# Attention and two expert layers on one core: merged q, k and v loads, another order of products at layer ends, silu in one operation

## Chip, cores and metric

One core of a Trainium2 chip runs the whole program in one launch. The metric is device time in microseconds (us), as the median of several executions.

## What is computed

```python
scores = scale * q @ k.T - log(S)          # (4, 12, 448, 64) each of q, k, v
attn   = 1 / (1 + exp(-scores))
x      = attn @ v                          # -> (1792, 768) rows: batch x sequence
xn     = x / sqrt(mean(x*x) + 1e-6) * rms_g
x      = (silu(xn @ w_gate) * (xn @ w_val)) @ w_out      # d_ff 1536
h      = x @ w_in
out    = (h - tanh(h)) @ w_out2                          # d_ff 2048
```

All arrays are fp32. The kernel splits every fp32 operand into a high and a low fp32r part and makes each product from three matmuls (high·high, high·low, low·high).

## The kernel before

**Stages.** Activations lie with features on the 128 partitions and the 448 tokens of one batch element along the free dimension. The attention works through 24 pairs of heads (4 batch elements, 6 pairs each). For a pair, `pair_load` (L490 to L520) brings q, k and v; `pair_prep` splits q and k (L279, L530); `scores` (L553) makes the scores of two heads in the two halves of the partitions; `sigmoid` (L563) is eight ScalarE operations; `pair_av` (L593, L599) multiplies by v, and `pair_end` copies the result out. After six pairs `norm` (L634, L644) works out the root mean square of a batch element.

Then come two layers, first for the batch elements 0 and 1 together, then for 2 and 3. The first matrix of a layer (phases Ag and Av for gate and value, C for the second layer) is multiplied by Strassen-Winograd's seven products over two rows of blocks and two batch elements: one *job* (`seven_units`, matmuls at L794) has 7 products of 3 steps `i` of 3 matmuls, 63 in all, and takes six PSUM banks; product 2 goes on top of product 1's bank. Step `i` needs the right-hand operands of feature chunks 2i and 2i+1 (B11, B21, B22 and the sums T1 to T4), which `right_units` makes (L675 sums, L279 and L670 split). `end` turns the results into activations: for the gate a ScalarE sigmoid (L742) and a multiplication by the value itself (L743), on VectorE or GpSimd. The second matrix (phases B and D, matmuls at L830) adds up groups of GR = 4 rows `k` of blocks over six columns `m`, a group of 4 jobs and 144 matmuls; `epilogue` (L721) adds each group's sum to an accumulator. The last group of phase B also calls `right_units` for phase C.

**Weights.** They come as int64 words holding an fp64 value; `load` (L317) fetches 768 KB, `convert` makes fp32 of it (ScalarE L333, L338, L342, then a clamp L345 and a shift-and-or L347), `factors` makes the sums (L413) and splits (L418) for a job, `whole_tile` the splits for B and D (L459). Converted weights are stored to DRAM for the second pass. The first six jobs' weights are converted beside the attention.

**What sets the order.** All work is recorded as units in a list; `Plan.issue` then simulates the five queues with written-down durations and takes, among the units that can start soonest (within 300 ns), the one recorded first. So each engine's instruction order is fixed when the program is built, and each engine runs it in order: an instruction that waits holds up all behind it, on SP (all DMA issues) too. The order of the blocks in B and D is the list `ORDER_1_OUT` or `ORDER_2_OUT`; in a job the order is this (L805 to L810, first job of a phase: `p == 0`):

```python
names = (1, 6, 7, 5, 2, 4, 3)
if p == 0:
    order = [(n, i) for n in names[:4] for i in range(2)] + [(n, 2) for n in names[:4]]
    order += [(n, i) for n in names[4:] for i in range(3)]
```

`right_a` (L868) makes the right-hand operands of phase A; for the second pass its units are spread beside the last jobs of the first one, where x is read back from DRAM. L279 is the helper `copy`, used for casts and for copies out of PSUM.

## Time and profile before

| what | us |
|---|---|
| median of 3 executions (1157.83 to 1166.39) | 1160.0 |
| the profiled execution | 1158.56 |
| its span, first to last instruction | 1156.8 |
| TensorE busy (96% of the span, 5574 records) | 1107.9 |
| VectorE busy (75%) | 865.2 |
| ScalarE busy (48%) | 558.2 |
| GpSimd busy (28%) | 321.9 |

The mean granted TensorE clock is 0.984 of full speed. A row of a timeline gives the start, the time taken, the engine, the source line, what it does and how many instructions were merged; in brackets stands the idle time ahead of it and what ended it. "SPq" is the queue that issues all DMAs. A few matmul records are missing from the trace, so a count there can be some short.

### The profile page before, as it was taken

What the parts mean: (1) busy time and instruction counts of PE and PEld (TensorE: products, weight loads), DVE (VectorE), ACT (ScalarE), POOL (GpSimd) and SP (SyncE); (2) the same over time, 40 slices, a digit from 0 to 9 for tenths busy, and PEclk for the clock granted to TensorE, in tenths of its full rate; (3) what the DMA queues carried; (4) which work ended last, traced back from release to release, by engine and by line L of the source; (5) the groups of instructions that cost most, each with busy time, mean ns of one, the idle gap of its engine ahead of it and who ended that gap; (6) DMA issues with size and microseconds to landing.
All of it is one profiled execution on the core that took longest, in us unless ns stands there. A gap on an engine that the chain in (4) does not pass through costs nothing. (4 is left out here: it accounts for less than half of the span.)

```text
span 1156.8 us, 15127 instructions
## 1 busy us (share of the span) xinstructions
PE 1107.9 (96%) x5574; PEld 943.8 (82%) x5574; DVE 865.2 (75%) x1347; ACT 558.2 (48%) x904; POOL 321.9 (28%) x203
## 2 busy tenths in 40 slices
PE   8798988999999997999999899999999999999998
PEld 4344443989999986899999789999999899999987
DVE  2566883796698899898999899948838899394642
ACT  4678996455476576676575424312303243121110
POOL 0003010253254232334444523322211324051300
PEclk9898999999999999999999899999999999999999
DMA  3777655234257463455556651221313113313203
GB/s 105 228 216 235 195 152 190 91 109 164 82 191 269 141 232 123 138 211 198 207 211 216 241 189 56 83 82 55 110 55 110 55 56 109 104 61 110 109 1 123
DMA packets 55322, 162.27 MB, mean 140 GB/s; under 512 B 13904, under 2 KB 30928, under 8 KB 55248
## 3 DMA queue, kind: packets, MB, share of 16 engines
q1 hardware_dynamic: 55248, 161.30, 41.4%
q8 instruction: 44, 0.72, 0.3%
q14 instruction: 30, 0.25, 0.1%
HBM read 115.27 MB, written 46.01 MB: 139 GB/s over the span
## 5 line engine op out<-in xcount | busy, mean ns | idle before, releaser
L794 PE MATMUL ps<-unit,wt 128*128 128x448 f32 x2160 | 454.9, 368 | 11.2 <-DVE unit L670 7.0
L794 PEld LDWEIGHTS ps<-unit,wt 128*128 128x128 f32 x2160 | 407.8, 189 | 49.6 <-DVE unit L670 7.8
L830 PE MATMUL ps<-unit,wt 128*128 128x448 f32 x2016 | 416.6, 367 | 8.2 <-DVE unit L279 7.3
L830 PEld LDWEIGHTS ps<-unit,wt 128*128 128x128 f32 x2016 | 379.7, 189 | 42.8 <-DVE unit L279 8.4
L765 DVE TENSOR_TENSOR unit<-ps,unit 128x448 f32<-128x448 f32 x240 | 142.6, 618 | 47.5 <-PE ps L794 44.0
L279 ACT COPY unit<-ps 128x448 f32<-128x448 f32 x86 | 45.8, 534 | 162.5 <-PE ps L794 90.0
L279 ACT CAST unit<-unit 128x448 fp32r<-128x448 f32 (+1 forms) x143 | 76.9, 567 | 86.0 <-DVE unit L721 22.0
L721 DVE TENSOR_TENSOR unit<-ps,unit 128x448 f32<-128x448 f32 x120 | 68.9, 616 | 60.9 <-PE ps L830 60.8
L345 POOL TENSOR_SCALAR cv<-cv 128x768 f32<-128x768 f32 x28 | 82.6, 2948 | 89.1 <-ACT cv L342 89.1
L563 ACT ACTIVATE unit<-ps 128x448 f32<-128x448 f32 x192 | 90.2, 543 | 5.4 <-PE ps L553 4.1
L279 ACT CAST wt<-cv 128x768 fp32r<-128x768 f32 x78 | 64.6, 833 | 57.2 <-PE ps L794 20.8
L553 PE MATMUL ps<-unit 64*128 64x448 f32 (+1 forms) x576 | 75.7, 397 | 14.3 <-ACT unit L279 5.0
L553 PEld LDWEIGHTS ps<-unit 64*128 64x128 f32 (+1 forms) x576 | 52.1, 182 | 42.9 <-issue 18.8
L794 PE MATMUL ps<-unit,cv 128*128 128x448 f32 x360 | 79.8, 366 | 0.0
L593 PE MATMUL ps<-unit 128*64 128x448 f32 x288 | 68.2, 607 | 9.3 <-ACT unit L563 9.2
L794 PEld LDWEIGHTS ps<-unit,cv 128*128 128x128 f32 x360 | 67.5, 188 | 5.6
L708 DVE TENSOR_TENSOR unit<-unit 128x448 fp32r<-128x448 f32 x89 | 66.5, 757 | 4.3 <-ACT unit L279 2.3
L418 POOL TENSOR_TENSOR wt<-cv,wt 128x768 fp32r<-128x768 f32 x21 | 41.6, 1980 | 100.2 <-ACT wt L279 56.7
L279 DVE CAST unit<-unit 128x448 fp32r<-128x448 f32 (+1 forms) x102 | 48.2, 473 | 28.2 <-DMA unit<-in_qkt 25.4
L342 ACT ACTIVATE cv<-wt 128x768 f32<-128x768 f32 x68 | 61.5, 906 | 10.5 <-DVE cv L347 3.9
L708 POOL TENSOR_TENSOR unit<-unit 128x448 fp32r<-128x448 f32 x23 | 26.8, 1169 | 138.0 <-DVE unit L279 130.2
L418 DVE TENSOR_TENSOR wt<-cv,wt 128x768 fp32r<-128x768 f32 x59 | 62.1, 1064 | 2.5 <-ACT wt L279 1.5
(71 smaller groups left out, 1020.7 us busy)
## 6 DMA issues: line engine op xcount, KB each, us to landing
wt<-in_w_out SPq DMA_DIRECT2D x28, 768.0 KB, 4.9
wt<-in_w_in SPq DMA_DIRECT2D x16, 768.0 KB, 5.9
wD<-wt SPq DMA_DIRECT2D x16, 768.0 KB, 4.1
wt<-wD SPq DMA_DIRECT2D x16, 768.0 KB, 4.2
wt<-in_w_gate SPq DMA_DIRECT2D x12, 768.0 KB, 5.4
wt<-in_w_val SPq DMA_DIRECT2D x12, 768.0 KB, 5.8
wB<-wt SPq DMA_DIRECT2D x12, 768.0 KB, 4.0
wt<-wB SPq DMA_DIRECT2D x12, 768.0 KB, 4.1
```

The costliest lines, as they stand in the source:

```text
L279: add(engines, lambda e: (nc.scalar.copy if e == "ACT" else nc.vector.tensor_copy)(to(), of()), reads, writes)
L342: add(act(NW), lambda e: nc.scalar.activation(t.tile, r.tile[:, :, 1].bitcast(F32), AF.Abs, scale=2.0 ** 16), [r["h"]], [t["t"]])
L345: add({**dve(NW, fast=True), **pool1(NW)}, lambda e: ENG[e].tensor_scalar(out=t.tile, in0=t.tile, scalar1=LOW, scalar2=HIGH, op0=ALU.max, ...
L418: add({**dve(n, psum=False), **pool(n)}, lambda e: ENG[e].tensor_sub(lo(), a(), hi().bitcast(F32)), [*ak, kh], [kl])
L553: nc.tensor.matmul(ps[i, c].tile[:n, :S], lhsT=f[w].tile[rows, c * P:c * P + n], rhs=f[q].tile[rows, :], start=(w, q) == ("kh", "qh"), sto ...
L563: add(act(S, psum=True), lambda e: nc.scalar.activation(to.tile[at:at + n, :S], ps.tile[:n, :S], AF.Sigmoid, bias=-math.log(S), scale=1.0 ...
L593: nc.tensor.matmul(ps.tile[i * D:(i + 1) * D, :S], lhsT=v.tile[:, n * D:(n + 1) * D], rhs=a.tile, start=(c == 0), stop=False)
L708: add({**pool(S), **dve(S, psum=False)}, lambda e: ENG[e].tensor_sub(c["l"].tile, t.tile, c["h"].tile.bitcast(F32)), [t["t"], kh], [kl])
L721: add(dve(S), lambda e: nc.vector.tensor_add(a.tile, psv(), a.tile), [ps["t"], a["t"]], [a["t"]])
L765: add(dve(S), lambda e: nc.vector.tensor_add(t.tile, banks[n].tile[:, :S], x.tile), [banks[n]["t"], x["t"]], [t["t"]])
L794: nc.tensor.matmul(ps.tile[:, :S], lhsT=part(a), rhs=x[b].tile, start=n not in ON_TOP and i == 0 and q == 0, stop=i == 2 and q == 2, skip_ ...
L830: nc.tensor.matmul(ps.tile[:, :S], lhsT=wt, rhs=a[p].tile, start=first and i == 0, stop=last and i == 2,)
```

## The change

- q and k of two heads are read as one DMA of 128 rows instead of two of 64; only the last 64 columns of k in batch elements 0 and 1 stay apart. v of a pair is one DMA for its first three chunks and one for the last. In batch elements 0 and 1 the last chunk is now read with its zero half. The first two weight loads no longer wait for the third pair's operands; the plan counts 3500 instead of 2000 ns until a weight load has landed.
- In B and D the last group runs the first three columns with its first two rows, the same columns with its last two rows, then the other three columns with four rows each. In a phase's first job the steps 0 and 1 of the products 1, 6, 7, 5, 4 and 3 come first, then all that need step 2 and product 2.
- `right_units` is made in two parts, for an even and an odd chunk, and recorded 60 places earlier for the plan's choice (`plan.lag`). The second pass's `right_a` ends one job earlier.
- silu is one ScalarE `Silu`; the multiplication L743 for it is gone. The clamp (L345) is VectorE's alone. The pools change: 79 instead of 81 units, 6 instead of 5 conversion buffers, and one instead of two `c` tiles among them.

```diff
-N_UNIT, N_MOE, N_WT, N_CV = 81, 44, 8, 5
+N_UNIT, N_MOE, N_WT, N_CV = 79, 44, 8, 6
+FIRST = 60
+def out_order(n):
+    half = GR // 2
+    order = [(k, m) for g in range(n // GR - 1) for m in range(KM) for k in range(g * GR, (g + 1) * GR)]
+    order += [(k, m) for ks in (range(n - GR, n - half), range(n - half, n)) for m in range(KM // 2) for k in ks]
+    return order + [(k, m) for m in range(KM // 2, KM) for k in range(n - GR, n)]
-ORDER_1_OUT = [(k, m) for g in range(KF1 // GR) for m in range(KM) for k in range(g * GR, (g + 1) * GR)]
+ORDER_1_OUT = out_order(KF1)
...
+        self.rank.append(n + self.lag)
...
-            finish, start, n, e, ns, uses_port = min((c for c in cands if c[1] <= soonest), key=lambda c: c[2])
+            finish, start, n, e, ns, uses_port = min((c for c in cands if c[1] <= soonest), key=lambda c: (self.rank[c[2]], c[2]))
...
-        "cv": (N_CV, {"cv": 2, "c": 2, "top": 1, "a22": 2}),
+        "cv": (N_CV, {"cv": 2, "c": 1, "top": 1, "a22": 2}),
...
-        add({"SP": (2200, False)}, lambda e: nc.sync.dma_start(out=r.tile, in_=SRC[ph][at]), reads, [r["l"], r["h"]], after=2000)
+        add({"SP": (2200, False)}, lambda e: nc.sync.dma_start(out=r.tile, in_=SRC[ph][at]), reads, [r["l"], r["h"]], after=3500)
...
-            add({**dve(NW, fast=True), **pool1(NW)}, lambda e: ENG[e].tensor_scalar(
+            add(dve(NW, fast=True), lambda e: ENG[e].tensor_scalar(
...
-            for i in range(2):
-                rows = slice(i * D, (i + 1) * D)
-                of = qkt[b * H + 2 * p + i][rows]
...
-                add({"SP": (1.4 * (hi - lo), False)}, lambda e, of=of, rows=rows, at=at: nc.sync.dma_start(
+            apart = w == "k" and hi > 3 * P and b < PAIRED
+            for i in range(2 if apart else 1):
+                rows = slice(i * D, (i + 1) * D) if apart else slice(0, P)
+                of = qk_rows[h * P + D:][rows, at + i * D:at + i * D + hi - lo]
+                add({"SP": (640 if apart else max(460, 1.45 * (hi - lo)), False)}, lambda e, of=of, rows=rows: nc.sync.dma_start(
...
-                if b % 2 and m % 2:
-                    for u in right_units("C", (b - 1, b), m // 2, xg):
+                if b % 2:
+                    plan.lag = -FIRST
+                    for u in right_units("C", (b - 1, b), m // 2, xg, m % 2):
                         u()
+                    plan.lag = 0
...
-            add(act(S, psum=psum), lambda e: nc.scalar.activation(sg.tile, of(), AF.Sigmoid), [x["t"]], [sg["t"]])
-            add(two, lambda e: ENG[e].tensor_mul(sg.tile, of(), sg.tile), [x["t"], sg["t"]], [sg["t"]])
+            add(act(S, psum=psum), lambda e: nc.scalar.activation(sg.tile, of(), AF.Silu), [x["t"]], [sg["t"]])
...
-            order = [(n, i) for n in names[:4] for i in range(2)] + [(n, 2) for n in names[:4]]
-            order += [(n, i) for n in names[4:] for i in range(3)]
+            free = [n for n in names if n not in ON_TOP]
+            order = [(n, i) for n in free for i in range(2)]
+            order += [(n, i) for n in names for i in range(3) if i == 2 or n in ON_TOP]
...
-        load(i, [pair_t[0, BEHIND]["ql"][0]] if (0, BEHIND) in pair_t else [])
+        load(i)
...
-    beside = [(last_c + 1, half_way, right_a(BATCHES[1], True))]
+    beside = [(last_c + 1, half_way - 1, right_a(BATCHES[1], True))]
```

The queue of SP at the program's start, before the change; `in_qkt` holds q and k, `in_vp` v in pairs, `ve` the last chunk of v:

```order
L500 DMA unit<-in_qkt 64x128 x2
L500 DMA unit<-in_qkt 64x448 x2
L500 DMA unit<-in_qkt 64x256 x2
L500 DMA unit<-in_qkt 64x64 x2
L511 DMA unit<-in_vp 128x384
L520 DMA ve<-in_vp 64x64 x2
L500 DMA unit<-in_qkt 64x384 x2
L500 DMA unit<-in_qkt 64x64 x2
L500 DMA unit<-in_qkt 64x448 x2
```

And with it, as far as the second pair's q:

```order
L513 DMA unit<-in_qkt 128x128
L513 DMA unit<-in_qkt 128x448
L513 DMA unit<-in_qkt 128x256
L513 DMA unit<-in_qkt 64x64 x2
L531 DMA unit<-in_vp 128x384
L533 DMA ve<-in_vp 128x128
L513 DMA unit<-in_qkt 128x384
L513 DMA unit<-in_qkt 64x64 x2
L513 DMA unit<-in_qkt 128x448
```

Up to the second pair's q, SP issued seventeen DMAs; now it issues eleven.

ScalarE around the last score sigmoids (L563 before, L576 now); L742 is the gate's sigmoid, L766 the gate's silu. Before:

```order
L279 COPY unit<-ps 128x448
L612 ACTIVATE unit<-unit 128x448
L563 ACTIVATE unit<-ps 128x448 x2
L563 ACTIVATE unit<-ps 64x448 x2
L279 COPY unit<-ps 128x448
L612 ACTIVATE unit<-unit 128x448
L279 COPY unit<-ps 128x448
L279 CAST wt<-cv 128x2x384
L742 ACTIVATE unit<-unit 128x448
L279 CAST wt<-cv 128x2x384
```

Now:

```order
L289 COPY unit<-ps 128x448
L623 ACTIVATE unit<-unit 128x448
L289 COPY unit<-ps 128x448
L766 ACT_TABLE_LOAD
L766 ACTIVATE unit<-unit 128x448
L576 ACT_TABLE_LOAD
L576 ACTIVATE unit<-ps 128x448 x2
L576 ACTIVATE unit<-ps 64x448 x2
L766 ACT_TABLE_LOAD
L766 ACTIVATE unit<-ps 128x448
```

Three table loads stand there that were not there before: one gate unit's silu has moved ahead of the last four sigmoids, and the table is changed for it, back, and again. Behind these rows no further load stands in the program.

VectorE at the end of phase B of the first pass, where the second layer begins: L721 (now L743) adds the last columns' sums, L675 and L670 (now L686 and L681) make the right-hand operands of the last two chunks; L345, L347, L413, L418 (now L355, L357, L423, L428) are weights. Before:

```order
L721 TENSOR_TENSOR unit<-ps,unit 128x448 x2
L347 SCALAR_TENSOR_TENSOR wt<-cv,wt 128x768
L721 TENSOR_TENSOR unit<-ps,unit 128x448 x2
L345 TENSOR_SCALAR cv<-cv 128x768
L347 SCALAR_TENSOR_TENSOR wt<-cv,wt 128x768
L413 TENSOR_TENSOR cv<-wt 128x384
L413 TENSOR_TENSOR cv<-cv,wt 128x384
L413 TENSOR_TENSOR cv<-wt 128x384
L413 TENSOR_TENSOR cv<-wt,cv 128x384
L418 TENSOR_TENSOR wt<-wt 128x768
L675 TENSOR_TENSOR unit<-unit 128x448 x3
L670 TENSOR_TENSOR unit<-unit 128x448 x7
```

Now:

```order
L423 TENSOR_TENSOR cv<-wt 128x384
L423 TENSOR_TENSOR cv<-cv,wt 128x384
L423 TENSOR_TENSOR cv<-wt 128x384
L423 TENSOR_TENSOR cv<-wt,cv 128x384
L428 TENSOR_TENSOR wt<-wt 128x768
L743 TENSOR_TENSOR unit<-ps,unit 128x448 x2
L686 TENSOR_TENSOR unit<-unit 128x448 x3
L681 TENSOR_TENSOR unit<-unit 128x448 x5
```

The weight work that stood between the last sums and the operands now stands ahead of the last sums.

## Rows read from the trace of the kernel before

**Rows 1.** Stretches: length, then PE, PEld, DVE, ACT, POOL busy, PEclk, DMA share, GB/s.

```profile
0.00:205.50 205.50, 179.72 (x1052) 92.29 (x1053) 121.21 (x220) 154.44 (x300) 19.01 (x19) 0.95 0.62 187
205.50:1152.60 947.10, 927.95 (x4524) 851.52 (x4522) 742.80 (x1125) 403.76 (x605) 302.86 (x184) 0.99 0.37 130
...
75.00:175.00 100.00, 91.61 (x567) 46.36 (x567) 78.45 (x142) 90.21 (x177) 14.70 (x11) 0.95 0.66 197
400.00:700.00 300.00, 284.79 (x1364) 259.99 (x1363) 275.73 (x414) 188.89 (x268) 113.32 (x58) 0.97 0.55 194
...
457.10:463.90 6.80, 4.13 (x11) 3.59 (x12) 6.39 (x12) 4.16 (x8) 0.00 (x0) 0.52 0.31 117
...
120.00:138.00 18.00, 17.85 (x122) 8.97 (x120) 15.71 (x29) 17.79 (x39) 1.01 (x1) 1.00 0.76 225
```

**Rows 2.** Timeline of TensorE in the attention.

```profile
14.06 2.61 PE L553 MATMUL ps<-unit 64*128 64x448 f32 x12 [2.27 <-DVE unit L279]
...
35.99 4.75 PE L593 MATMUL ps<-unit 128*64 128x448 f32 x12 [5.51 <-ACT unit L563]
...
120.09 2.69 PE L553 MATMUL ps<-unit 64*128 64x448 f32 x24
...
126.16 2.72 PE L553 MATMUL ps<-unit 64*128 64x448 f32 x24
...
183.59 0.92 PE L553 MATMUL ps<-unit 64*128 64x448 f32 x5 [4.08 <-ACT unit L563]
```

**Rows 3.** Timeline of ScalarE in the attention.

```profile
34.61 0.89 ACT L333 ACTIVATE wt<-wt 128x768 uint32<-128x768 uint16 x1 [5.58 <-DMA wt<-in_w_gate]
...
181.29 0.89 ACT L333 ACTIVATE cv<-wt 128x768 uint32<-128x768 uint16 x1 [5.17 <-DMA wt<-in_w_out]
```

**Rows 4.** Timeline of SP's queue, at the start and in the attention.

```profile
0.72 5.03 SPq L500 DMA_DIRECT2D unit<-in_qkt  x8
...
145.67 1.19 SPq L520 DMA_DIRECT2D ve<-in_vt  x2
...
148.57 3.67 SPq L500 DMA_DIRECT2D unit<-in_qkt  x6
152.28 0.58 SPq L317 DMA_DIRECT2D wt<-in_w_out  x1
```

**Rows 5.** TensorE's waits: total us, how many, the longest.

```profile
PE ps L830 <- DVE unit L279: 7.3, 3, 4.3
PE ps L794 <- DVE unit L670: 7.0, 2, 6.7
...
PE ps L794 <- DVE wt L418: 2.8, 2, 1.9
```

**Rows 6.** Timeline of TensorE in the layers.

```profile
459.77 6.32 PE L794 MATMUL ps<-unit,wt 128*128 128x448 f32 x20 [6.74 <-DVE unit L670]
...
752.78 29.34 PE L830 MATMUL ps<-unit,wt 128*128 128x448 f32 x144
781.96 3.41 PE L794 MATMUL ps<-unit,wt 128*128 128x448 f32 x16
```

**Rows 7.** Timeline of VectorE at the end of phase B, first pass.

```profile
451.98 1.15 DVE L721 TENSOR_TENSOR unit<-ps,unit 128x448 f32<-128x448 f32 x2
...
457.50 1.69 DVE L675 TENSOR_TENSOR unit<-unit 128x448 f32<-128x448 f32 x3
```

**Rows 8.** Groups of instructions: busy us, mean ns of one, idle before and its releaser.

```profile
L345 POOL TENSOR_SCALAR cv<-cv 128x768 f32<-128x768 f32 x28 | 82.6, 2948 | 89.1 <-ACT cv L342 89.1
L345 DVE TENSOR_SCALAR cv<-cv 128x768 f32<-128x768 f32 x40 | 23.0, 575 | 15.2 <-ACT cv L342 15.1
L742 ACT ACTIVATE unit<-unit 128x448 f32<-128x448 f32 x36 | 20.4, 576 | 36.2 <-DVE unit L765 36.1
L743 DVE TENSOR_TENSOR unit<-unit 128x448 f32<-128x448 f32 x27 | 20.1, 760 | 4.1 <-ACT unit L742 3.7
L888 ACT ACT_TABLE_LOAD x1 | 1.3, 1283 | 0.7 <-PEq L990 0.7
```

More of the change, by code (lines that the diff above doesn't have):

```diff
@@ L70, in __init__ @@
     def __init__(self, room):
-        self.room, self.work = room, []
+        self.room, self.work, self.rank, self.lag = room, [], [], 0
     def add(self, engines, run, reads=(), writes=(), stream=None, after=0):
@@ L508, in pair_load @@
+        if (b, p) == (0, 0):
+            parts = ("k", 0, P), ("q", 0, S), ("k", P, 3 * P), ("k", 3 * P, S)
+        elif b < PAIRED:
+            parts = ("k", 0, 3 * P), ("k", 3 * P, S), ("q", 0, S)
+        else:
+            parts = ("k", 0, S), ("q", 0, S)
+        for w, lo, hi in parts:
+            load(w, lo, hi)
+        v, end = vs_t[b, p] = unit("vs"), slot("ve", ve_p, [P, 2, D], F32, "ve")
+        hv = h - PAIRED * H
         if b < PAIRED:
-            of = vp[b * HP + p]
-            ends = [of[i * D:(i + 1) * D, 3, i] for i in range(2)]
@@ L511, in pair_load @@
-            add({"SP": (550, False)}, lambda e: nc.sync.dma_start(
-                out=v.tile[:, :6 * D].rearrange("p (c i d) -> p c i d", c=3, i=2), in_=of[:, :3]), [], [v[0], v[1]], after=2000)
-        else:
-            of = [vt[(b - PAIRED) * H + 2 * p + i] for i in range(2)]
-            ends = [of[i][i * D:(i + 1) * D, 3] for i in range(2)]
-            for i in range(2):
-                add({"SP": (280, False)}, lambda e, i=i: nc.sync.dma_start(
-                    out=v.tile[:, 3 * i * D:3 * (i + 1) * D].rearrange("p (c d) -> p c d", c=3), in_=of[i][:, :3]), [], [v[i]], after=2000)
@@ L519, in pair_load @@
-        for i in range(2):
-            add({"SP": (90, False)}, lambda e, i=i: nc.sync.dma_start(out=end.tile[i * D:(i + 1) * D], in_=ends[i]), [], [end[i]], after=2000)
+            of, rest, to, n = vp[b * HP + p][:, :3], vp[b * HP + p][:, 3], lambda: end.tile, "c i"
+        else:
+            of, rest, to, n = vt[hv:hv + 2, :, :3].rearrange("i p c d -> p i c d"), vt_rows[hv * P + D:][:P, 3], lambda: end.tile[:, 0], "i c"
+        add({"SP": (550, False)}, lambda e: nc.sync.dma_start(
+            out=v.tile[:, :6 * D].rearrange(f"p ({n} d) -> p {n} d", i=2, c=3), in_=of), [], [v["t"]], after=2000)
@@ L522, in pair_prep @@
+        add({"SP": (460, False)}, lambda e: nc.sync.dma_start(out=to(), in_=rest), [], [end["t"]], after=2000)
     def pair_prep(b, p):
@@ L573, in pair_qk @@
                     t = a_t[b, 2 * p + i, c] = unit("s")
-                    sigmoid(ps[i, c], P, t)
+                    sigmoid(ps[i, c], t)
             else:
@@ L598, in rest @@
                 rows = slice(i * D, (i + 1) * D)
-                nc.tensor.matmul(ps.tile[rows, :S], lhsT=v_end.tile[rows], rhs=end.tile[rows, :S], start=False, stop=True)
-        add({"PE": (12 * MM + 150, False)}, halves, [v[0], v[1], *[a["t"] for x in two for a in x]], [ps["t"]], stream="attention")
-        add({"PE": (4 * MM, False)}, rest, [v_end[0], v_end[1], end[0], end[1]], [ps["t"]], stream="attention")
+                nc.tensor.matmul(ps.tile[rows, :S], lhsT=v_end.tile[rows, i if b < PAIRED else 0], rhs=end.tile[rows, :S], start=False, stop=True)
+        add({"PE": (12 * MM + 150, False)}, halves, [v["t"], *[a["t"] for x in two for a in x]], [ps["t"]], stream="attention")
+        add({"PE": (4 * MM, False)}, rest, [v_end["t"], end[0], end[1]], [ps["t"]], stream="attention")
     def pair_end(b, p):
```

60 lines of the change are left out of this document (32 added, 28 removed).

## The prediction

> **What bounds the kernel now.** I read the stretches first, then the timelines of the engines that wait in each. The program has two parts with different limits, and they part near 205.5 us, where the last pair of the attention is through and 30 matmuls of the layers have been done in between.
>
> In the layers TensorE is the bound. A group of phase B or D shows its pace where nothing is late: 144 matmuls from 752.78 to 781.96 us, 202.6 ns each [rows 6]. Over both passes the layers have 14 such groups and 40 jobs of 63 matmuls, 4536 matmuls in all; 4506 of them stand in the second stretch, which at this pace are 913 us. The stretch takes 947.1 us [rows 1]. The missing 34 us are few and large: three waits of 7.3 us in all where a layer's second matrix begins its last group and the last job's activations aren't ready (a copy or cast on VectorE, L279, comes last), one of 6.7 us where the second layer's first job waits for its operands (L670), two of 2.8 us for weights (L418) [rows 5]; and behind the long ones the granted clock stays at the lower of its two levels (1.2 instead of 2.4 GHz) for a while: 0.52 over the 6.8 us from 457.1 us on, so about 3.3 us of work lost [rows 1]. The longest of the three, 4.3 us, is followed by a second such spell of the same length; a third, half as long, follows a wait for weights.
>
> In the attention TensorE is busy 179.7 of 205.5 us, at a clock of 0.95 [rows 1], but not bound by its own work: where nothing is late, a pair takes 6.07 us (from 120.09 to 126.16 us [rows 2]), 24 pairs 145.7 us. Two others run beside it. ScalarE is busy 154.4 us of the stretch, 90.2 of the 100 us from 75 to 175 us, and nearly all of 120 to 138 us, where TensorE never waits [rows 1]. SP's queue is as full: from 145.67 to 152.28 us it issues ten loads of one pair and one store without a pause, 6.6 us or 0.60 us each, and only then a weight load [rows 4]; TensorE needs 6.07 us for a pair. So weight loads leave late, and ScalarE, which runs in order, stands before a conversion whose words haven't landed: 5.58 us at 29 us, 5.17 us at 176 us [rows 3]; score sigmoids queue behind it, and TensorE waits 5.51 and 4.08 us for those [rows 2].
>
> **The loads.** A pair of the batch elements 0 and 1 had 9 DMAs and gets 6, one of 2 and 3 had 10 and gets 4: 12 times 3 and 12 times 6, and one more for the first pair, which is 109 issues less. By the first row of [rows 4] one takes 5.03 / 8 = 0.63 us of SP, so some 68 us leave a queue that is full for about 180 us. A pair with store and weight load then takes SP some 6 x 0.60 = 3.6 us, well under TensorE's 6.07: SP is no bound any more. At the start the second pair's q is issued eleventh instead of seventeenth, 6 x 0.63 = 3.8 us earlier, and the wait of 2.27 us at 14.06 us goes. The bytes hardly change and the DMA engines are 62% busy in this stretch [rows 1], so there is room. The first two weight loads still stand behind the fifth pair in SP's order, so the missing wait lets nothing jump ahead. The plan's 3500 ns put conversions later on ScalarE, which is the other cure for the waits of [rows 3].
>
> What it is worth is bounded by what is late next, ScalarE. Its 154.4 us, and two table loads of 1.28 us [rows 8] that now stand before the last sigmoids, are 157 us; the first sigmoid can't start before about 6 us. If ScalarE were busy 99% of the time, as from 120 to 138 us, the stretch would take 6 + 157 / 0.99 = 165 us and 41 us would go; with the 90% of 75 to 175 us, which still has late loads in it, 6 + 157 / 0.90 = 180 us and 25 us; if nothing but TensorE's two waits of 2.27 and 5.51 us and the 3.4 us of half speed behind the second went, 11 us. I take **29 us**, nearer to the 90%, since work of other kinds still gets between the sigmoids in the order.
>
> **The layer ends.** With the last group's first three columns cut in two, 3 x 2 x 2 x 3 = 36 matmuls (7.3 us at 202.6 ns) come before the last job's activations are read, instead of 12 (2.4 us). The longest wait was 4.3 us, the cover grows by 4.9 us, so the three waits go, **7.3 us**, and the half speed behind the longest, **3.3 us**. In the first job of a layer 36 matmuls come before step 2 instead of 24, and product 1 needs only B11 of the last two chunks, which comes from the column before the last; T2 is needed after 39 matmuls, 7.9 us. VectorE's order shows it ready by then: behind the last sums (1.15 us) there stood 4.4 us of weight work before L675 (453.1 to 457.5 us [rows 7]); now L686 and L681 follow at once, so sums, T2, a cast and a split take about 4 us. The weight work now ahead of the last sums may hold them up by some 3 us, which still fits in 7.9. So **6.7 us** and **3.3 us** of half speed go too. Bounds: nothing, if VectorE's backlog arrives whole at the same place, and all 34 us of the stretch if the weights' waits go as well. I count no gain for the second pass's earlier x.
>
> **silu, the clamp, the pools.** 48 silus replace 48 sigmoids: no row has a Silu; the nearest is the gate's sigmoid, 576 ns [rows 8], and ScalarE is busy under half of the layers, so even twice that is hidden. The multiplications go (27 of 760 ns on VectorE, 20.1 us, and others on GpSimd or from PSUM). The 28 clamps that GpSimd took 2948 ns for now take VectorE 575 ns each, 16.1 us more [rows 8]. VectorE gets no fuller, and the clamp's chain gets 2.4 us shorter 28 times; only one `c` tile means the conversions of B's and D's weights can't overlap. I set these off against each other. The three table loads fall at the end of the attention: two are in the sum above, the third delays a silu by **1.3 us**, which TensorE meets with layer products still to do. For waits that appear in new places I take off **2 us**.
>
> Here a rule of the Trainium skill speaks against the change: its page "ScalarE: Activation LUTs", section "What ACT_TABLE_LOAD costs", says that each switch to another set costs a drain of about 1.38 us beside the load's 1.28 us, and asks for activations to be grouped by set. The one load of this trace takes 1283 ns, as the page has it, but nothing ran ahead of it, so no row shows a drain. By the page three switches would cost 8.0 us on ScalarE instead of 3.8, and the sum would be some 4 us higher.
>
> **The sum.** 29 + 7.3 + 3.3 + 6.7 + 3.3 - 1.3 - 2 = 46.3 us. The profiled execution took 1158.6 us, so 1158.6 - 46.3 = **1112 us**; the median of the runs shown, 1160.0, lies 1.4 us above it.
>
> **Rivals.**
> - *ScalarE keeps the attention slow.* Casts, copies and conversions stand between the sigmoids as before, and only the 11 us of the start go: 11 + 17 = 28, so 1130 us. For it: 90% busy already. Against it: the idle rest stands just ahead of late loads [rows 3].
> - *The layer ends give nothing.* VectorE is 92% busy from 400 to 700 us (275.7 of 300 [rows 1]); the weight work that is now ahead of the sums comes late there, and TensorE waits a little further on: only the 29 us, 1130 us.
> - *Both go as far as they can.* 41 + 21, so 1097 us.
> - *Slower: weights late in the first pass.* 42 jobs of it have their weights converted beside the layers (14 of the first matrices, 28 of the second). They have some 50 us less time for it, VectorE gets 28 clamps, and one `c` tile serializes the chain. If each job waited as long as the longest wait for weights now, 1.9 us [rows 5], that were 80 us, and 1192 us; it decides from 47 / 42 = 1.1 us a job. Against it: only two of these jobs wait now, and VectorE loses more in multiplications than it gains.
> - *The change does less than it says.* k's last columns of 12 pairs are still two DMAs, and the silus need three table loads; both are counted above.
>
> **Chances.** The forecast 0.60, ScalarE 0.14, the layer ends 0.10, both to the end 0.10, weights late 0.06. The forecast's own range is 1100 to 1125 us; to hold 8 in 10 it reaches to the two rivals at 1130 with some room, since both can happen together in part (11 + 7 less would be 1140), and to 1097 below: 1094 to 1140 us. A measurement of this kernel tells about 1%, 11.6 us, from no change: faster than that is all but the last rival and the worst of the two at 1130 together, 0.88; within it 0.07; slower 0.05.
>
> **What would show it.** In the new profile the last pair should end near 175 us, with ScalarE without waits for weight loads over 2 us; SP's queue should have pauses; TensorE should show no wait of over 1 us at the start of a last group, and none of over 1 us at the second layer's first job; three table loads of 1.28 us near the end of the attention. The prediction is wrong if TensorE's waits for L418's successor (weights) add up to over 10 us, or if the attention still ends near 200 us.

## The result, and the profile after

The changed kernel takes 1124.36 us (median of 4 executions, 1121.55 to 1125.98) against 1158.91 us for the kernel before in the same comparison (4 executions, 1155.02 to 1166.39): a ratio of 0.9692 [0.9638, 0.9746]. (The ratios here are those of the means, with a 95% interval; the medians differ by 34.6 us, 3.0%.) It is faster. The forecast was 46.3 us less and 1112 us, with a range of 1094 to 1140 us, so the time lies inside the range and 12 us above the forecast. The profiled execution took 1123.12 us, 35.4 us less than that of before.

From the page: the busy time of the engines, and the granted clock in forty slices.

```profile
PE 1091.8 (97%) x5574; PEld 939.2 (84%) x5574; DVE 838.4 (75%) x1343; ACT 552.7 (49%) x902; POOL 219.5 (20%) x164
PEclk9999999999999998999999989999999999999999
```

TensorE's share hardly changes (96% before), so shares tell little; the gain has to be looked for in two stretches. Two numbers split it. The last product with v of the attention ends at 203.1 us before (first row) and at 187.6 us after (second row):

```profile
202.12 0.97 PE L599 MATMUL ps<-unit,ve 64*64 64x448 f32 x4
```

```profile
186.60 0.97 PE L610 MATMUL ps<-unit,ve 64*64 64x448 f32 x4
```

By then 18 and 57 layer matmuls are done; taking off 0.2026 us for each of those [rows 6], the attention costs 199.4 and 176.0 us, **23.4 us less**. What is left until the last matmul, less 0.2026 us for each of the other layer matmuls, is called the layers' loss: 34.4 and 22.3 us, **12.1 us less**. Together 35.5 us, the whole difference of the two profiled executions. The split is bookkeeping: where a plan does layer work between two pairs, its ScalarE work counts as attention.

TensorE's waits, whole program (total us, how many, the longest), against [rows 5]:

```profile
PE ps L817 <- ACT unit L289: 7.7, 1, 7.7
PE ps L817 <- DVE unit L743: 3.7, 1, 3.7
...
PE ps L817 <- DVE wt L428: 1.6, 1, 1.6
...
PE ps L604 <- ACT unit L576: 0.6, 2, 0.3
```

L817 (before L794) are the jobs, L854 (before L830) the groups of B and D, L604 (before L593) the products with v. The waits of L830 are gone without a successor. The products with v, which had waited up to 5.51 us for score sigmoids [rows 2], now wait 0.6 us for them in all. But a job still waits 7.7 us, and a wait of 3.7 us is new.

SP's queue in the attention (start, us, what), against [rows 4]:

```profile
70.48 0.33 SPq L533 DMA_DIRECT2D ve<-in_vp  x1
70.85 0.91 SPq L513 DMA_DIRECT2D unit<-in_qkt  x2
71.80 0.43 SPq L531 DMA_DIRECT2D unit<-in_vt  x1
72.65 0.34 SPq L367 DMA_DIRECT2D wAg<-wt  x1
73.03 0.43 SPq L327 DMA_DIRECT2D wt<-in_w_gate  x1
76.79 0.33 SPq L533 DMA_DIRECT2D ve<-in_vt  x1
```

With a pair of the batch elements 2 and 3 SP now has four loads, a store and a weight load to issue; they are through after 3 us, and 3.3 us of pause follow. In the attention ScalarE has no wait for a weight load left (two of over 5 us before [rows 3]). The windows show how full the engines are now (length, PE, PEld, DVE, ACT, POOL busy, PEclk, DMA share, GB/s); the first row is the whole attention, the second its middle, the third VectorE's worst stretch of [rows 1], and the last two are the spells of low clock at the two waits:

```profile
0.00:187.60 187.60, 176.00 (x1080) 92.93 (x1080) 127.22 (x239) 160.64 (x306) 7.05 (x12) 0.96 0.63 206
...
25.00:150.00 125.00, 116.44 (x737) 59.31 (x739) 96.92 (x183) 118.81 (x227) 6.54 (x6) 0.96 0.73 243
...
400.00:700.00 300.00, 286.59 (x1387) 263.62 (x1386) 274.72 (x435) 171.43 (x256) 67.46 (x47) 0.97 0.51 179
...
430.70:441.00 10.30, 6.04 (x15) 5.03 (x16) 10.05 (x17) 7.52 (x12) 0.00 (x0) 0.52 0.20 74
...
659.83:663.30 3.47, 3.47 (x9) 3.12 (x10) 3.43 (x6) 0.00 (x0) 0.00 (x0) 0.51 0.54 198
```

From 25 to 150 us ScalarE is busy 118.8 of 125 us, 95%, and is the fullest engine of the attention (TensorE 93%). From 150 us to the end of the attention it is TensorE: 37.58 of 37.60 us at full clock, with ScalarE at 26.93, as layer products fill it there. VectorE is as full in the layers as it was, 274.7 of 300 us against 275.7.

ScalarE at the end of the attention, where the load of a new function table stands three times:

```profile
179.59 1.28 ACT L766 ACT_TABLE_LOAD   x1
181.81 0.58 ACT L766 ACTIVATE unit<-unit 128x448 f32<-128x448 f32 x1 [0.94 <-DVE unit L788]
182.41 1.28 ACT L576 ACT_TABLE_LOAD   x1
183.70 1.96 ACT L576 ACTIVATE unit<-ps 128x448 f32<-128x448 f32 x4
185.68 1.28 ACT L766 ACT_TABLE_LOAD   x1
186.97 0.54 ACT L766 ACTIVATE unit<-ps 128x448 f32<-128x448 f32 x1
```

TensorE at the start of the second layer and of the second pass:

```profile
418.57 5.36 PE L817 MATMUL ps<-unit,wt 128*128 128x448 f32 x24
...
434.69 0.74 PE L817 MATMUL ps<-unit,wt 128*128 128x448 f32 x1 [7.72 <-ACT unit L289]
435.70 6.30 PE L817 MATMUL ps<-unit,wt 128*128 128x448 f32 x17 [0.27 <-DVE unit L681]
...
655.01 1.08 PE L817 MATMUL ps<-unit,wt 128*128 128x448 f32 x4 [1.62 <-DVE wt L428]
659.83 2.61 PE L817 MATMUL ps<-unit,cv 128*128 128x448 f32 x6 [3.73 <-DVE unit L743]
```

And VectorE ahead of the first of these. Phase B's last matmul ended at 418.7 us; the L743 at 432.24 us adds its last two sums:

```profile
421.62 0.61 DVE L743 TENSOR_TENSOR unit<-ps,unit 128x448 f32<-128x448 f32 x1
...
425.51 0.55 DVE L355 TENSOR_SCALAR cv<-cv 128x768 f32<-128x768 f32 x1
...
431.37 0.94 DVE L428 TENSOR_TENSOR wt<-wt 128x768 fp32r<-128x768 f32 x1
432.24 1.14 DVE L743 TENSOR_TENSOR unit<-ps,unit 128x448 f32<-128x448 f32 x2
433.42 1.70 DVE L686 TENSOR_TENSOR unit<-unit 128x448 f32<-128x448 f32 x3
435.03 2.76 DVE L681 TENSOR_TENSOR unit<-unit 128x448 fp32r<-128x448 f32 x5
```

The last sums start 13.5 us after the last matmul: 2.9 us of weight work until 421.62, 3.9 us of earlier sums and operands, and 6.7 us of weight work (425.51 to 432.24) directly ahead of them. VectorE has no gap there; it is late. Job one of the second layer ran the 39 matmuls that need nothing of these sums, stood still from 426.97 to 434.69 us, and then ran at the lower clock until 441 us (0.52 from 430.7 us on).

Three groups answer to [rows 8]:

```profile
L854 PE MATMUL ps<-unit,wt 128*128 128x448 f32 x2016 | 410.8, 365 | 0.0
L355 DVE TENSOR_SCALAR cv<-cv 128x768 f32<-128x768 f32 x68 | 38.0, 559 | 20.8 <-ACT cv L352 20.7
L766 ACT ACTIVATE unit<-unit 128x448 f32<-128x448 f32 x36 | 20.4, 576 | 31.5 <-DVE unit L788 31.4
```

B and D have no idle time ahead of any matmul. All 68 clamps are on VectorE, at 559 ns. A silu takes 576 ns, exactly what the sigmoid took.

### The profile page after: what moved, and what is told of

The parts are those of the page before. It is cut to its first block, busy times and chain, and to the rows that moved or that the text cites. A ratio compares the mean times of both kernels' runs of the same rounds, so it can differ in the third digit from the quotient of the medians.

```text
span 1121.3 us, 14895 instructions
## 1 busy us (share of the span) xinstructions
PE 1091.8 (97%) x5574; PEld 939.2 (84%) x5574; DVE 838.4 (75%) x1343; ACT 552.7 (49%) x902; POOL 219.5 (20%) x164
## 4 chain that ended last, share of the span: by engine, by line
PE 54%; DVE 7%; ACT 1%; issue 0%; DVEq 0%; ACTq 0%
PE ps L817 30%; PE ps L854 24%; DVE unit L681 2%; DVE unit L686 1%; DVE unit L743 1%; DVE unit L719 1%; DVE wt L428 1%; ACT unit L289 0%; DVE unit L730 0%; DVE cv L357 0%; DVE wt L357 0%; DVE cv L423 0%; DVE unit L774 0%; DVE unit L289 0%; DVE cv L355 0%
## 5 line engine op out<-in xcount | busy, mean ns | idle before, releaser
L817 PE MATMUL ps<-unit,wt 128*128 128x448 f32 x2160 | 453.8, 368 | 11.1 <-ACT unit L289 7.7
L817 PEld LDWEIGHTS ps<-unit,wt 128*128 128x128 f32 x2160 | 407.9, 189 | 47.2 <-ACT unit L289 8.3
L854 PE MATMUL ps<-unit,wt 128*128 128x448 f32 x2016 | 410.8, 365 | 0.0
L854 PEld LDWEIGHTS ps<-unit,wt 128*128 128x128 f32 x2016 | 378.8, 188 | 29.8
L289 ACT COPY unit<-ps 128x448 f32<-128x448 f32 x91 | 47.8, 534 | 179.9 <-PE ps L817 112.4
L743 DVE TENSOR_TENSOR unit<-ps,unit 128x448 f32<-128x448 f32 x120 | 69.3, 616 | 63.1 <-PE ps L854 62.8
L289 ACT CAST unit<-unit 128x448 fp32r<-128x448 f32 x132 | 70.7, 565 | 65.6 <-DVE unit L686 23.6
L289 ACT CAST wt<-cv 128x768 fp32r<-128x768 f32 x75 | 62.4, 835 | 70.6 <-PE ps L817 25.7
L576 ACT ACTIVATE unit<-ps 128x448 f32<-128x448 f32 x192 | 90.1, 543 | 8.3 <-PE ps L566 7.1
L817 PE MATMUL ps<-unit,cv 128*128 128x448 f32 x360 | 81.9, 370 | 3.7 <-DVE unit L743 3.7
L730 DVE TENSOR_TENSOR unit<-unit 128x448 fp32r<-128x448 f32 x94 | 74.7, 810 | 6.1 <-ACT unit L289 4.0
L817 PEld LDWEIGHTS ps<-unit,cv 128*128 128x128 f32 x360 | 68.1, 190 | 10.8 <-DVE unit L743 4.1
L566 PE MATMUL ps<-unit 64*128 64x448 f32 (+1 forms) x576 | 71.5, 386 | 5.5 <-DVE unit L289 2.4
L566 PEld LDWEIGHTS ps<-unit 64*128 64x128 f32 (+1 forms) x576 | 49.4, 176 | 32.2 <-issue 15.4
L289 ACT CAST wt<-wt 128x768 fp32r<-128x768 f32 x33 | 27.6, 837 | 81.7 <-PE ps L854 34.6
L604 PE MATMUL ps<-unit 128*64 128x448 f32 x288 | 64.1, 579 | 0.7 <-ACT unit L576 0.6
L428 DVE TENSOR_TENSOR wt<-cv,wt 128x768 fp32r<-128x768 f32 x61 | 60.8, 1007 | 2.9 <-ACT wt L289 2.2
L289 DVE CAST unit<-unit 128x448 fp32r<-128x448 f32 (+2 forms) x113 | 49.5, 438 | 16.1 <-DMA unit<-in_qkt 13.6
L428 POOL TENSOR_TENSOR wt<-cv,wt 128x768 fp32r<-128x768 f32 x19 | 36.3, 1911 | 111.6 <-ACT wt L289 87.7
L355 DVE TENSOR_SCALAR cv<-cv 128x768 f32<-128x768 f32 x68 | 38.0, 559 | 20.8 <-ACT cv L352 20.7
```

The costliest lines, as they stand in the source:

```text
L289: add(engines, lambda e: (nc.scalar.copy if e == "ACT" else nc.vector.tensor_copy)(to(), of()), reads, writes)
L355: add(dve(NW, fast=True), lambda e: ENG[e].tensor_scalar(out=t.tile, in0=t.tile, scalar1=LOW, scalar2=HIGH, op0=ALU.max, op1=ALU.min), [t[ ...
L428: add({**dve(n, psum=False), **pool(n)}, lambda e: ENG[e].tensor_sub(lo(), a(), hi().bitcast(F32)), [*ak, kh], [kl])
L566: nc.tensor.matmul(ps[i, c].tile[:n, :S], lhsT=f[w].tile[rows, c * P:c * P + n], rhs=f[q].tile[rows, :], start=(w, q) == ("kh", "qh"), sto ...
L576: add(act(S, psum=True), lambda e: nc.scalar.activation(to.tile[at:at + n], ps.tile[:n, :S], AF.Sigmoid, bias=-math.log(S), scale=1.0 / ma ...
L604: nc.tensor.matmul(ps.tile[i * D:(i + 1) * D, :S], lhsT=v.tile[:, n * D:(n + 1) * D], rhs=a.tile, start=(c == 0), stop=False)
```

## The experiments

The kernels ran in three groups, each with the kernel before beside it (1157.75 us for e1 to e4, 1157.06 for e5 to e12, 1156.08 for e13 to e16). Attention and loss are worked out of each one's profile as above.

| kernel | median us | ratio [95%] | attention | layers' loss | of it slow pace |
|---|---|---|---|---|---|
| before | 1158.91 | 1 | 199.4 | 34.4 | 4.3 |
| the change | 1124.36 | 0.9692 [0.9638, 0.9746] | 176.0 | 22.3 | 0.3 |
| e1 loads alone | 1133.94 | 0.9791 [0.9759, 0.9824] | 169.6 | 40.6 | 3.6 |
| e2 layer ends alone | 1159.17 | 1.0003 [0.9976, 1.003] | 205.5 | 29.8 | 8.7 |
| e3 sigmoid again | 1129.14 | 0.9767 [0.9729, 0.9805] | 176.4 | 34.4 | 13.4 |
| e4 clamp on two engines | 1129.3 | 0.9756 [0.9728, 0.9784] | 177.9 | 27.2 | 5.3 |
| e5 old first job | 1130.0 | 0.9764 [0.9739, 0.979] | 176.8 | 28.2 | 4.6 |
| e6 sums earlier | 1124.38 | 0.9719 [0.9675, 0.9764] | 178.0 | 27.0 | 9.1 |
| e11 no lead | 1122.35 | 0.9712 [0.9676, 0.9749] | 176.1 | 21.0 | 0.8 |
| e12 loads cut in two | 1146.06 | 0.9908 [0.9877, 0.994] | 194.9 | 30.6 | 9.2 |
| e13 casts on ScalarE | 1125.49 | 0.9719 [0.9677, 0.976] | 174.7 | 21.6 | 0.3 |
| e14 squares off ScalarE | 1124.67 | 0.9727 [0.968, 0.9774] | 171.0 | 26.2 | 4.5 |
| e15 both | 1119.09 | 0.9678 [0.9628, 0.9728] | 170.5 | 21.8 | 0.3 |
| e16 both, sums earlier | 1117.47 | 0.9658 [0.961, 0.9706] | 172.6 | 17.6 | 0.3 |

In some profiles TensorE went through part of the layers at a pace 2% slower, at full granted clock (last section). The last column is what that adds to the loss: the time above 202.6 ns, summed over neighbouring matmuls whose starts lie 190 to 215 ns apart, from the last product with v on. The profile of before has 4.3 us of it, that of the changed kernel 0.3 us. As the pace differs between profiles for no known reason, losses are best compared without this column: 30.1 us before, 22.0 us with the change, **8.1 us less**.

**e1, the loads alone**, on the kernel before:

```diff
-        add({"SP": (2200, False)}, lambda e: nc.sync.dma_start(out=r.tile, in_=SRC[ph][at]), reads, [r["l"], r["h"]], after=2000)
+        add({"SP": (2200, False)}, lambda e: nc.sync.dma_start(out=r.tile, in_=SRC[ph][at]), reads, [r["l"], r["h"]], after=3500)
...
-                of = qkt[b * H + 2 * p + i][rows]
...
+                of = qk_rows[h * P + D:][rows, at + i * D:at + i * D + hi - lo]
...
-        load(i, [pair_t[0, BEHIND]["ql"][0]] if (0, BEHIND) in pair_t else [])
+        load(i)
```

> The kernel before with the change's loads alone: merged q, k and v DMAs, no wait of the first weight loads for the third pair, 3500 ns in the plan. Theory (SP's full queue held the attention back): the attention gives what it gave in the changed kernel, some 23 us, so 1134 to 1139 us; the last pair ends before 185 us; the waits at the last groups of B and D stay at about 7 us. Rival (the attention was held by ScalarE's own work, and the 23 us came from the order of other units): less than 10 us, 1150 us or more.

1133.94 us, 23.8 less than before in its group. The attention went from 199.4 to 169.6: 29.8 us less, where the prediction had put 29. The layers kept their waits, the last groups too:

```profile
PE ps L797 <- DVE unit L673: 10.8, 3, 8.4
PE ps L833 <- DVE unit L279: 5.3, 4, 2.1
```

So the loads carry the attention's gain. Alone they give none in the layers, whose loss is 6.2 us higher; 29.8 - 6.2 = 23.6 us is what the time shows. The rest of the change, put on top of the loads, is worth the 9.6 us between this median and the changed kernel's.

**e2, the layer ends alone**: the orders, the two-part `right_units` with its lead, the first job, the earlier x.

```diff
+FIRST = 60
...
-ORDER_1_OUT = [(k, m) for g in range(KF1 // GR) for m in range(KM) for k in range(g * GR, (g + 1) * GR)]
+ORDER_1_OUT = out_order(KF1)
...
+            order = [(n, i) for n in free for i in range(2)]
```

> The kernel before with the layer ends alone: new order of blocks and of a phase's first job, operands in two parts with the lead of 60, right_a ending one job earlier; loads, silu, clamp and pools as before. Theory (the ends' waits go, but the wait of the second layer's first job stays, and a new wait for a bank comes up at the second pass): 8 to 14 us less, 1145 to 1151 us; no wait at L830's successor, one of over 4 us at the second layer's first job. Rival (the ends are worth all they were counted at, 17 us or more): 1142 us or less, and no wait over 2 us at the first jobs.

1159.17 us (median of ten executions, 1150.83 to 1164.86): no gain, and neither side expected that. TensorE's waits:

```profile
PE ps L817 <- ACT unit L289: 5.9, 1, 5.9
PE ps L563 <- ACT unit L664: 5.4, 1, 5.4
```

The last groups have no wait here either, so the new order does that part by itself. The second layer's first job waits 5.9 us, with none of the change's loads, silu or clamp in it (6.7 us before [rows 5]): the new layer ends don't remove that wait. The loss without slow pace is 21.1 us, 9.0 us less than before, so the layer ends give in the layers all that the whole change gives there. Two things hide it in this profile: 4.4 us more of slow pace than in that of before, and the attention, whose own units this edit doesn't touch, took 6.1 us more. The plan is made anew for the whole program, and the scores now wait 5.4 us for a copy of the norm (L664), which was 1.0 us at the most before. An edit at one place is not neutral at the others.

**e3, sigmoid and multiplication again:**

```diff
-            add(act(S, psum=psum), lambda e: nc.scalar.activation(sg.tile, of(), AF.Silu), [x["t"]], [sg["t"]])
+            add(act(S, psum=psum), lambda e: nc.scalar.activation(sg.tile, of(), AF.Sigmoid), [x["t"]], [sg["t"]])
+            add(two, lambda e: ENG[e].tensor_mul(sg.tile, of(), sg.tile), [x["t"], sg["t"]], [sg["t"]])
```

> The changed kernel with silu as before: a ScalarE sigmoid and a multiplication on VectorE or GpSimd; no table load but the first. Theory (silu is hidden, the three table loads cost TensorE nothing): within 5 us of the changed kernel, 1119 to 1130 us. Rival (VectorE is the bound of the first pass, so 48 multiplications back cost time): 1132 us or more, with longer waits at the first jobs. Second rival (the table loads cost TensorE what they take): 3 to 4 us less, 1120 us.

1129.14 us, 4.8 above the changed kernel, with intervals that overlap. The extra table loads are gone, the waits of 7.7 and 3.7 us stay, and the attention is 176.4 as against 176.0: the loads of the tables cost the attention nothing that can be seen. silu is worth 0 to 5 us; the profiles, without slow pace, show no difference (1123.0 us here, 1122.8 us for the change).

**e4, the clamp on two engines** (VectorE or GpSimd, as before the change):

```diff
-            add(dve(NW, fast=True), lambda e: ENG[e].tensor_scalar(
+            add({**dve(NW, fast=True), **pool1(NW)}, lambda e: ENG[e].tensor_scalar(
...
```

> The changed kernel with the clamp open to GpSimd again, as before. Theory (the wait at the second layer's first job comes from weight work that stands ahead of the last sums, whoever clamps): that wait stays above 5 us, and the time within 5 us of the changed kernel, 1119 to 1130 us. Rival (VectorE is late because the 28 clamps were given to it): the wait falls under 3 us, and with the lower clock behind it 8 to 12 us go, 1112 to 1116 us.

1129.3 us. The first wait of the second layer is 5.1 us instead of 7.7, one for weights 2.8 instead of 1.6, that of 3.7 us stays. So the clamp accounts for 2.6 of the 7.7 us at the most, and isn't the main thing that makes VectorE late.

**e5, the old order of a first job:**

```diff
-            order = [(n, i) for n in free for i in range(2)]
-            order += [(n, i) for n in names for i in range(3) if i == 2 or n in ON_TOP]
+            order = [(n, i) for n in names[:4] for i in range(2)] + [(n, 2) for n in names[:4]]
+            order += [(n, i) for n in names[4:] for i in range(3)]
```

> The changed kernel with the order of products in a phase's first job as before (products 1, 6, 7, 5 with steps 0 and 1, then their step 2, then 2, 4, 3). Theory (the wait of 3.7 us at the second pass comes from products 4 and 3 wanting all six banks within 36 matmuls, while the banks of the last sums are still full): no wait for a bank over 1 us there, but the wait at the second layer's first job gets 2 to 3 us longer, as step 2 comes 12 matmuls earlier; 1120 to 1130 us in all. Rival (the sums are late on VectorE whatever the order wants): the bank wait stays above 3 us.

1130.0 us. The wait of 3.7 us is gone: it comes from the new order, which wants six banks within its first 36 matmuls, while phase D's last sums still have to empty theirs. (With the same order that wait was 1.0 us in e2, so it also depends on when VectorE gets to these sums.) In return the second layer's first job waits 9.9 us instead of 7.7.

**e6, the last group's sums 60 places earlier in the plan:**

```diff
+            plan.lag = -FIRST * last
             add(dve(S), lambda e: nc.vector.tensor_add(a.tile, psv(), a.tile), [ps["t"], a["t"]], [a["t"]])
+            plan.lag = 0
```

> The changed kernel, in which the sums of the last group of B and D are also taken 60 places earlier by the plan, ahead of weight work. Theory (both waits that are left come from these sums standing behind other VectorE work): the wait of 7.7 us at the second layer's first job falls under 2 us, the bank wait of 3.7 us goes, and with the lower clock behind both 12 to 18 us less than the changed kernel, 1106 to 1113 us. Rival (VectorE has too much work there, and weights come late instead): waits for weights grow by as much, 1120 us or more.

1124.38 us, the changed kernel's time. The sums are in time now, the waits of 7.7 and 3.7 us are gone, and the same job waits for its weights instead:

```profile
PE ps L819 <- ACT wt L289: 5.5, 1, 5.5
PE ps L856 <- ACT wt L289: 2.9, 2, 2.0
```

ScalarE's casts (L289) that the first of these waits names start at 426.62 us, 0.1 us behind a sum of weights on VectorE (L423) that now stands behind the operands. The waits have become smaller, though: the loss without slow pace is 17.9 us instead of 22.0, and a longer attention takes 2.0 us of that back. Mostly, the order on the engine chooses who waits for VectorE's arrears.

**e11, no lead for the operands:**

```diff
-FIRST = 60
+FIRST = 0
```

> The changed kernel without the lead of 60 places for the operands of phase C. Theory (the lead puts the operands behind the last sums at once, but the sums themselves are late, so the lead is worth little): within 6 us of the changed kernel, 1118 to 1130 us, the wait at the second layer's first job between 6 and 12 us. Rival (the lead is what shortens that wait): the wait over 12 us, and 1132 us or more.

1122.35 us, with waits of 7.1 us at the second layer's first job and of 3.0 us in the second pass. The 60 places are worth nothing that can be measured.

**e12, every load of 128 rows of q and k, the last chunk of v, and v of the batch elements 2 and 3 cut in two**: the same bytes, 206 instead of 121 issues for the loads; the order of every other engine is unchanged.

```diff
-                    out=t[w].tile[rows, lo:hi], in_=of), [], [t[w]["t", lo, i]], after=2000)
...
+                    if rows.stop - rows.start == P:
+                        for r in (slice(0, D), slice(D, P)):
+                            nc.sync.dma_start(out=t[w].tile[r, lo:hi], in_=of[r])
...
```

> The changed kernel with every 128-row load of q and k, the last chunk of v and v of the batch elements 2 and 3 issued as two DMAs of half the rows each, 206 issues of q, k and v instead of 121; the order of all other engines is word for word that of the changed kernel. Theory (SP's full queue held the attention back): 85 x 0.60 = 51 us more on SP, of which SP has some 50 us free in the changed kernel's attention in all but not at the places where it counts: the attention gets 8 to 25 us longer, 1132 to 1150 us. Rival (the gain of the attention came from the plan's order and the 3500 ns, not from the number of issues): within 5 us of the changed kernel.

1146.06 us, 21.7 more than the changed kernel; the attention takes 194.9 instead of 176.0, so 18.9 of the 23.4 us are lost again. First TensorE's longest group of waits, then SP's queue:

```profile
PE ps L620 <- ACT unit L592: 10.4, 7, 4.7
```

```profile
68.57 1.23 SPq L518 DMA_DIRECT2D unit<-in_qkt  x2
69.85 1.23 SPq L516 DMA_DIRECT2D unit<-in_qkt  x2
71.13 0.58 SPq L539 DMA_DIRECT2D unit<-in_vp  x1
```

SP issues without a pause again, 0.6 us each, and the waits for score sigmoids are back (L592 here). As nothing but the number of issues (and the size of each transfer) differs, this is the strongest evidence for the prediction's mechanism. How much comes back need not be what before lost, as this order was planned for the fewer issues.

**e13, casts and splits only on ScalarE**, to take load off VectorE (the same edit at three places):

```diff
-        copy({**act(S), **dve(S, fast=True)}, lambda: c["h"].tile, lambda: t.tile, [t["t"]], [kh])
+        copy(act(S), lambda: c["h"].tile, lambda: t.tile, [t["t"]], [kh])
```

> The changed kernel, in which the casts of weights and of activations to their high parts are ScalarE's alone (they were ScalarE's or VectorE's); the casts of q, k and the right-hand operands stay free. Theory (the waits that are left come from a VectorE that is full in the first pass): VectorE's share from 400 to 650 us falls, the waits at the second layer's first job and at the second pass fall by half or more, and 5 to 12 us go, 1112 to 1119 us. Rival (they come from the place of single units in the order, whatever VectorE's share): the wait of 7.7 us stays above 5 us, 1120 us or more.

1125.49 us, no gain. VectorE's busy time from 400 to 650 us falls from 230.4 to 219.6 us, yet the two waits are 7.1 and 4.7 us. Eleven us of freed time somewhere in 250 don't help at one place where the order is fixed.

**e14, the norm's squares on GpSimd or VectorE instead of ScalarE** (at two places):

```diff
-            add({**pool(S), **act(S)}, lambda e: square(e, sq.tile), [x["t"]], [sq["t"]])
+            add({**pool(S), **dve(S, psum=False)}, lambda e: square(e, sq.tile), [x["t"]], [sq["t"]])
```

> The changed kernel with the squares for the norm on GpSimd or VectorE instead of GpSimd or ScalarE. Theory (ScalarE is what bounds the attention now): some 22 squares of 0.5 us leave ScalarE, the attention gets 5 to 10 us shorter, 1114 to 1120 us. Rival (TensorE's own work and its waits for norms bound it): under 3 us, 1121 us or more.

1124.67 us, no gain in the median, but in the profile the attention takes 171.0 us, 5.0 less. ScalarE's share falls to 115.2 of 125 us, VectorE's rises by 9.9 us:

```profile
25.00:150.00 125.00, 116.68 (x754) 59.51 (x752) 106.78 (x200) 115.16 (x220) 4.83 (x4) 0.97 0.74 250
```

The layers take none of it back: their loss is 3.9 us higher, but 4.2 us more of it is slow pace. Whether the squares brought the 5.0 us is not shown. This plan also does only 6 layer matmuls instead of 57 before the last pair is through, as e1's does, and has one table load for silu instead of three. Against e1, with the same 6, ScalarE is busy 6.8 us less until the last product with v (147.8 and 154.6 us), and the attention is no shorter (171.0 and 169.6).

**e15, e13 and e14 together**:

> The two edits before together: casts in the layers on ScalarE alone, squares off ScalarE. If both theories hold their gains add up, 1102 to 1114 us; if neither does, 1120 us or more.

1119.09 us, 5.3 us below the changed kernel's median, with intervals that overlap. Attention 170.5, loss 21.8. That is e14's profile without its slow pace (171.0 and 21.7), so the casts add nothing that can be seen.

**e16, e15 and e6 together**:

> The two edits together, and the last groups' sums 60 places earlier in the plan. Theory (with VectorE less full the earlier sums no longer make weights late): both waits at the first jobs under 2 us without new waits for weights over 2 us, 1095 to 1110 us. Rival (the wait moves to the weights again, as with the earlier sums alone): no better than the two edits without it.

1117.47 us (1113.83 to 1122.51), the lowest median of all, 6.9 us below the changed kernel. Its ratio's interval [0.961, 0.9706] overlaps the changed kernel's [0.9638, 0.9746], so this is a candidate, not a shown improvement over the change; against the kernel before it is 3.4% faster. The wait has moved to the weights again, and a bank still comes late:

```profile
PE ps L819 <- ACT wt L289: 6.0, 1, 6.0
...
PE ps L819 <- DVE unit L790: 3.0, 1, 3.0
```

## Why the prediction was right, and where its terms were off

**The attention (forecast 29, measured 23.4; the loads alone 29.8).** The mechanism was right: SP's queue was full, weight loads left late, ScalarE stood before conversions, and TensorE waited for sigmoids. e1 has the gain with nothing else changed, and e12 takes most of it away again with nothing but the loads cut in two. The step's size for what comes next, ScalarE, fits e1: busy 122.7 of the 125 us from 25 to 150 us, and 154.6 us in all, which by the step's formula is 154.6 / (170.8 - 6) = 94%, where its 29 us stand for 157 / (205.5 - 29 - 6) = 92%. The changed kernel gets 6.4 us less than e1, and there the formula was off twice: ScalarE has 160.6 us of work until 187.6 us instead of 157, and is busy 160.6 / (187.6 - 6) = 88%. It is the fullest engine only up to 150 us (95% from 25 us on); the last 37.6 us are TensorE's. The plan does 57 layer matmuls before the last pair is through, e1's does 6, and the ScalarE work that goes with them (casts, copies, a silu between two table loads) lies before the end. No run moved that layer work alone, and e14, which lost it together with the squares, can't tell the two apart, so how the 6.4 us divide stays open. That ScalarE's work sets the length of the attention is likely from these shares, but not shown.

**The last groups (forecast 7.3 + 3.3).** Right in the waits: all three are gone, L854 has an idle time of 0.0 us, and e2 shows that the new order alone does it. The 3.3 us for half speed were too many. The spell of 6.8 us that [rows 1] show from 457.1 us on began while TensorE still waited (until 459.77 us [rows 6]); only the 4.1 us behind that ran at half speed, which is 2.1 us lost. The other place where the step used the figure is alike (wait until 657.81 us, a spell of 6.8 us from 655.3 us on, 2.1 us lost). At both it counted the part inside the wait once more.

**The second layer's first job (forecast 6.7 + 3.3, measured -1.0 and no gain in clock).** This is the step that failed, in the mechanism and not only in size: "The weight work now ahead of the last sums may hold them up by some 3 us, which still fits in 7.9." The block ahead of them was 6.7 us long, and VectorE came to it with 6.8 us of other work in arrears, so the sums started 13.5 us after the last matmul and not some 3. The cover of 39 matmuls (7.9 us) worked as counted; the first operands that were missing came at 434.7 us, 16.0 us after phase B's last matmul. The forecast read from VectorE's order what stands where, which was right, but counted as if VectorE were at the last sums when the last matmul ends. It was not even before the change, where the second layer began at 447.81 us and the last sums at 451.98 us [rows 7], 4.2 us later:

```profile
447.81 5.23 PE L794 MATMUL ps<-unit,wt 128*128 128x448 f32 x25
```

With these 4.2 us the step's own 3 and 4 us come to 11 and no longer fit in 7.9; that could have been read from the trace of before. This is the second rival at this one place: the wait doesn't go, it comes a little further on. e6 shows the same from the other side: once the sums are put earlier the weights are late, by 5.5 us. e13 shows that VectorE's total isn't the lever.

**New waits (forecast 2).** Mis-sized: 3.7 us for a bank at the second pass's first job, and 1.7 us of half speed behind it (0.51 over 3.5 us). It was in the edit itself: six banks in 36 matmuls instead of four in 24, and e5, with the old order, takes it away. The 1.6 us for weights are less than the 2.8 us before.

**The layers in all (forecast 46.3 - 29 = 17.3, measured 12.1).** Idle time of TensorE in them fell from 19.1 to 13.9 us, half speed (by the spells behind waits) from some 5.9 to 4.9 us. A further 4.0 us came from the slow pace in before's profiled execution; they are luck and no merit of the change, which leaves 8.1 us, under half of the forecast. Some 2 us weren't traced to a place.

**silu, the clamp, the pools (forecast 0, less 1.3 for a table load).** A silu takes what a sigmoid took, 576 ns, and e3 and e4 show 0 to 5 us each for silu and the clamp; intervals of this width can't tell more. The pools were not tried alone. On the table loads the trace decides: a switch to another table and its first use cost 1.28 us, with 0.02 us from the end of the activation ahead (182.39) to the load (182.41) and 0.01 us behind it (183.69 to 183.70). The Trainium skill, page "ScalarE: Activation LUTs", section "What ACT_TABLE_LOAD costs", adds a drain of about 1.38 us to each switch; none of the three switches here shows one, so ScalarE didn't lose the 4 us that this rule adds.

**The rivals.** Weights late in the first pass: 1.6 us in one job, so nothing near the 1.1 us a job from which it would have decided. ScalarE keeping the attention slow: in small part. The layer ends giving nothing: at one of the three places. Of the forecast's signs two were not seen: the second layer's first job, which was to show no wait of over 1 us, waits 7.7 us, and the attention ends at 187.6 instead of near 175 us; 7.9 of these 12.6 us are 39 layer matmuls more in it. The pauses on SP, ScalarE without waits for weight loads in the attention, the last groups without waits and the three table loads were seen. The time lies inside the range because the two parts fell short by no more than 5.6 and 5.2 us, the second with 4.0 us of luck in the pace.

## What to carry to other kernels

Count issues per queue against the pace of the engine that they feed: here a queue with 6.6 us of issues per 6.07 us of work was the bound, and merging DMAs paid although the bytes stayed the same. Where an order is fixed when the program is built, moving one piece of work ahead moved most of the wait to whoever stood behind it, as the engine was in arrears at that place; read the arrears there, from the trace (how long after its releaser does an instruction run), before counting a wait as gone. When a spell of low clock overlaps a wait, count only the part behind the wait. And before a loss of a few us is put down to an edit, look whether the matmuls without waits ran at the same pace in both profiles.

## What the runs showed that was not expected

TensorE has a second pace at full granted clock. A group of 144 matmuls with no wait in it takes 29.35 us in most places and 29.92 us in others, in the same program. Before the change (timeline of TensorE), an early and a later group:

```profile
266.69 29.92 PE L830 MATMUL ps<-unit,wt 128*128 128x448 f32 x144
...
498.87 29.35 PE L830 MATMUL ps<-unit,wt 128*128 128x448 f32 x144
```

In e3, where the early ones are quick and all from 469 us on are slow:

```profile
389.80 29.35 PE L855 MATMUL ps<-unit,wt 128*128 128x448 f32 x144
...
469.79 29.92 PE L855 MATMUL ps<-unit,wt 128*128 128x448 f32 x144
```

The windows before the change, 300 to 350 and 550 to 600 us, hold 244 and 249 matmuls, both at a granted clock of 1.00:

```profile
300.00:350.00 50.00, 50.00 (x244) 45.42 (x243) 43.35 (x67) 34.40 (x48) 22.83 (x14) 1.00 0.46 158
...
550.00:600.00 50.00, 50.00 (x249) 46.35 (x247) 46.73 (x67) 31.62 (x43) 21.84 (x11) 1.00 0.62 220
```

The difference is 2% (some 206.5 instead of 202.6 ns a matmul), it lasts for up to hundreds of us, and in these profiles it isn't tied to a place in the code. Where it holds over most of an execution, as in e3's profile (1136.37 us, its three other executions 1128.18 to 1129.69), it adds up to 13.4 us. It may be a good part of the scatter of some 10 us between executions of one kernel, of which only the profiled one has a trace; its cause is not known.
